# Padding the SBUF pools of a retention + maxout + bilinear kernel, so that stationary and moving operands of its matmuls start at other addresses

## The chip, the cores and the metric

The kernel runs on one core of one Trainium2 chip. The metric is the device time of one execution in microseconds. Three runs of the kernel before are given: 1272.45, 1270.91 and 1267.66 us, median 1270.91.

## What is computed

Three layers stand one behind the other, on 4608 tokens (8 batches of 576), model width 512:

```python
ret = (q @ k.T / sqrt(64)) * Dmat          # 8 heads; Dmat[i, j] = gamma_h ** (i - j) for i >= j, else 0
x = ret @ v                                 # retention; heads side by side: x is 4608 x 512
h = maximum(maximum(x @ w1, x @ w2), x @ w3)    # 512 -> 768
z = h @ w_out                               # 768 -> 512
g = (z @ u1) * (z @ u2)                     # 512 -> 1024, the second layer's w1 and w2
out = (g @ u3) @ u_out                      # 1024 -> 1024 -> 512
```

All is float32 (the weights come as float64 bits and are converted on the chip).

## The kernel before

TensorE takes the operands as float32r. For float32 accuracy each number is split into a high part (`copy_r`, L92, on ScalarE) and a low part (`low`, L95, a subtraction on VectorE or GpSimd), and each product becomes three matmuls, high x high, low x high and high x low, added up in PSUM. A matmul has a **stationary** operand of 128 x 128 (loaded into the array ahead of it by a LDWEIGHTS) and a **moving** one of 128 x 512 or 128 x 256 that is streamed through. In the profile a matmul row is named output<-moving,stationary, and the weight load has a row of its own on the queue PEld.

The program runs in five stages. Their matmuls are nearly all the work of TensorE:

1. **First products** (`products`, L478, matmul at L486), with the attention worked in between. Stationary: the tiles `w1h`/`w1l` (L197). Moving: `xh`/`xl` (L298), a block of 512 tokens; a few early ones are halved to 256 columns. 1896 matmuls of 512 columns and 96 of 256. An order written out by hand (`ORDER`) and a list of due times set the order.
2. **z** (`product`, matmul at L715, called in the loop over `z_groups`). Seven Strassen-Winograd products per group of two token blocks. Stationary: `zp["w"]` (`za11h` and so on, L545). Moving: `hh`/`hl`, split by `split_h` (L605). 504 matmuls of 512 columns; the last, half-sized group has 126 of 256.
3. **Fold** of u3 and u_out into one weight (output `ps_w`). Stationary `th`/`tl` (`get_w3t`, L720), moving `oh`/`ol` (`get_wo2`, L725), all in the pool `t34`. 192 matmuls of 512 columns.
4. **g** (outputs `ps_x`, `ps_v`, `ps_y`). Stationary: `piece` tiles of the pool `ws` (L658). Moving: two operand sets (`operand_set`, L797), set 0 in the pool `op0` on the right side of SBUF and set 1 in `op1` on the left side (L905); the token groups take them in turn. 1344 matmuls of 512 columns, half with each set, and 336 of 256 columns (the half-sized group, set 0).
5. **Out** (`add_o`, L1200). Stationary: `a11h` and so on (L1035). Moving: the folded weight's pieces. 1512 matmuls of 256 columns.

Where a tile lies in SBUF follows from the order in which pools and tiles are opened: on the left side each tile starts where the one before it ends, counted up from byte 640 of the partition; on the right side counted down from byte 229344. So an unused tile ahead of others moves them all. The kernel before has such paddings already: `skew` (L113) makes one, behind operand set 0 (L801, 352 bytes) and ahead of the stationary tiles of the stage out (L1034, 64 or 32 bytes). A half-sized group starts 48 columns into its tile (`columns`, L116), which are 192 bytes.

```python
def skew(pool, size):
    pool.tile([P, size // 4], F32, name="skew")

def columns(size):
    at = 0 if size == N1 else 48
    return slice(at, at + size)
```

Of the kernel before, what the change touches and what calls it, by code (L numbers as in the profile page):

```python
# [9 lines left out]
F32 = mybir.dt.float32  # L10
# [12 lines left out]
P = 128  # L23
# [64 lines left out]
def tile_retention_maxout_bilinear(ctx: ExitStack, tc, a, out):  # L88
# [3 lines left out]
    def copy_r(dst, src):  # L92
        nc.scalar.activation(dst, src, AF.Copy)  # L93

    def low(eng, dst, full, hi):  # L95
        eng.tensor_tensor(dst, full, hi.bitcast(F32), ALU.subtract)  # L96
# [13 lines left out]
    g_d = [dram.tile([P, KF2, N1], F32, name=f"g_d{t}") for t in range(NT // N1)]  # L110
    w4_d = dram.tile([P, KF2, DM], F32, name="w4_d")

    def skew(pool, size):  # L113
        pool.tile([P, size // 4], F32, name="skew")

    def columns(size):  # L116
        at = 0 if size == N1 else 48
        return slice(at, at + size)
# [2 lines left out]
        return ps_mm.tile([P, 512], F32, tag="mm", name=name)  # L121

    left = ctx.enter_context(ExitStack())
    hb_p = left.enter_context(tc.tile_pool(name="hb", bufs=4, side="left"))
    w1_p = left.enter_context(tc.tile_pool(name="w1", bufs=1, side="left"))
    x_p = {2: left.enter_context(tc.tile_pool(name="x2", bufs=1, side="left"))}
    cv_x = ctx.enter_context(ExitStack())
    x_p.update({t: cv_x.enter_context(tc.tile_pool(name=f"x{t}", bufs=1, side="left")) for t in range(2)})
    cv = cv_x.enter_context(tc.tile_pool(name="cv", bufs=2, side="left"))
# [372 lines left out]
    for t in range(n_blk):  # L502
        for f in range(KF1):
            for i in range(3):
                k = T_BLK * t + 3 * f + i
                if t < EARLY:
                    split = t == 0 and 3 * f + i < HALVED
                    for e, cols in enumerate(halves if split else (whole,)):
                        name = f"{t}.{3 * f + i}" + "ab"[e] * split
# [12 lines left out]
    zp = {}  # L522
# [7 lines left out]
    def splitter(pool, src, hi, lo, eng, tag, bufs):  # L530
        raw = pool.tile([P, hi.shape[-1]], F32, tag=tag, name=tag, bufs=bufs)
        load(raw, src)

        def split():
            copy_r(hi, raw)
            low(eng, lo, raw, hi)

        return split

    def open_z():  # L540
        right.close()
        cv_x.close()
        zp["ps"] = ctx.enter_context(tc.tile_pool(name="ps_2", bufs=2, space=PSUM, side="right"))
        p = zp["p"] = bx.enter_context(tc.tile_pool(name="zp", bufs=1, side="right"))
        zp["w"] = {x: [p.tile([P, KH, half], F32R, name=f"z{x}{v}") for v in "hl"] for x in AN}  # L545

    def raw_h(tag, bufs=1):
        return zp["p"].tile([P, KH, N1], F32, tag=tag, name=tag, bufs=bufs)
# [56 lines left out]
    def split_h(n):  # L605
        j, n = divmod(n, len(Z_ORDER))
        if j < len(z_groups):
            x = Z_ORDER[n][1]
            raw, size = hr[j, x], z_groups[j][3]
            hh, hl = hq[j, n] = [zp["p"].tile([P, KH, N1], F32R, tag=f"h{v}", name=f"h{v}", bufs=Z_RING)[:, :, columns(size)] for v in "hl"]  # L610
            copy_r(hh, raw)
            low(nc.vector, hl, raw, hh)

    t_last = T_BLK * (n_blk - 1)
    when(t_last, open_z)
    for c, tag in enumerate(("T3", "T2", "b21")):
        for n, step in enumerate(z_weights(c, tag)):
# [7 lines left out]
    for n in range(Z_RING):  # L625
        when(t_last + 13.6 + n, split_h, n)
    when(t_last + 15.2, load_h, 1, "b11")

    with tc.manual_schedule():
# [88 lines left out]
        t34, w3t, wo2 = {}, {}, {}  # L718
# [4 lines left out]
            return splitter(t34["p"], flat(w3t_d[:, k, 4 * e:4 * e + 4]), *map(flat, w3t[n]), nc.vector, "raw34", 3)  # L723

        def get_wo2(k):  # L725
            wo2[k] = [t34["p"].tile([P, DM], F32R, tag=x, name=x) for x in ("oh", "ol")]
            return splitter(t34["p"], wo2_d[:, k], *wo2[k], nc.gpsimd if k % 2 else nc.vector, "raw34", 3)

# [2 lines left out]
        def prepare_34(*gets):  # L731
            for split in pending:
                split()
            pending[:] = [get(n) for get, n in gets]

        first_34 = [((get_w3t, 0), (get_wo2, 0)), ((get_w3t, 1),), ((get_w3t, 2), (get_wo2, 1)), ()]

        def open_34():
            t34["p"] = t34x.enter_context(tc.tile_pool(name="t34", bufs=2, side="left"))

        zo_p = bx.enter_context(tc.tile_pool(name="zo", bufs=1, side="right"))

# [16 lines left out]
        for j, (_, _, _, size) in enumerate(z_groups):  # L759
            Z = {}  # L760
            saved = {}
            for n, (x, y) in enumerate(Z_ORDER):
                bank_of = "XVXYXYX"[n]
                fresh = bank_of not in Z
                if fresh:
                    Z[bank_of] = [bank8(f"ps_{bank_of}{i}") for i in range(2)]
                ps = Z[bank_of]
                ah, al = zp["w"][x]
                bh, bl = hq.pop((j, n))
                for i in range(2):  # L770
                    ms = slice(i * P, i * P + P)
                    product(ps[i][:, :size], [(ah[:, c, ms], al[:, c, ms], bh[:, c], bl[:, c]) for c in range(KH)], fresh, True, not fresh)
                for i in range(2):
                    if n in (0, 2, 3):
                        saved[n, i] = snap_z(ps[i], size)
                    elif n == 6:
                        keep_z(j, 2 + i, 0, ps[i])
                    else:
                        keep_z(j, *{1: (i, 0), 4: (2 + i, 1), 5: (i, 1)}[n], ps[i], saved.pop(({1: 0, 4: 3, 5: 2}[n], i)))
                split_h(j * len(Z_ORDER) + n + Z_RING)  # L780
                for fn, dj, *args in behind_z[n]:
                    fn(j + dj, *args)
                if steps and n in (2, 3, 5, 6):
                    steps.pop(0)()
            if j == 3:
                for step in steps:
                    step()
                sx.close()
                open_34()
                steps = [lambda gets=gets: prepare_34(*gets) for gets in first_34]  # L790
# [4 lines left out]
        BN = ("b11", "b21", "b22", "t1", "t2", "t3", "t4")  # L795

        def operand_set(pool, tag):  # L797
            return {x: [pool.tile([P, 2, N1], F32R, name=f"{x}{v}{tag}") for v in "hl"] for x in BN}

        ops = [operand_set(o_p, 0)]  # L800
        skew(o_p, 352)  # L801
        behind = []

# [79 lines left out]
        for n in range(2 * KF2):  # L883
            k, e = divmod(n, 2)
            th, tl = w3t.pop(n)
            for m in range(4 * e, 4 * e + 4):
                if k == 0:
                    ps_w.append(bank8(f"ps_w{m}"))
                product(ps_w[m], [(th[:, m % 4], tl[:, m % 4], *wo2[k])], k == 0, k == KF2 - 1)
                if k == KF2 - 1:  # L890
                    t = w4_p.tile([P, DM], F32, tag="w4", name="w4")
                    copy_r(t, ps_w[m])
                    load(w4_d[:, m], t)
            prepare_34(*[(get_w3t, n + 3)] * (n + 3 < 2 * KF2), *[(get_wo2, k + 2)] * (e == 1 and k + 2 < KF2))
            lows()
            if steps:
                steps.pop(0)()
# [5 lines left out]
        wk = ctx.enter_context(tc.tile_pool(name="wk", bufs=1, side="left"))  # L903
        cx = ctx.enter_context(ExitStack())
        ops.append(operand_set(cx.enter_context(tc.tile_pool(name="op1", bufs=1, side="left")), 1))  # L905

        def work(tag, bufs):
# [110 lines left out]
        def g_steps(s):  # L1018
# [13 lines left out]
            def split(x, eng):  # L1032
                if s in (0, 3) and not ops:
                    skew(gpool[s % 2], 32 if s else 64)  # L1034
                h, l = ops[x] = [gpool[s % 2].tile([P, 4, P], F32R, tag=f"{x}{v}", name=f"{x}{v}") for v in "hl"]  # L1035
                src = w[x]
                copy_r(h, src)
                if s:
                    low(eng, l, src, h)
                else:  # L1040
                    behind.append(lambda: low(eng, l, src, h))
# [58 lines left out]
        for n, (k, q) in enumerate(visits):  # L1100
            B, size = ops[k % 2], z_groups[k][3]
# [190 lines left out]
```

## Time and profile before

| what | value |
|---|---|
| runs | 1267.66, 1270.91, 1272.45 us |
| the profiled execution's own time | 1266.24 us |
| its span, first to last instruction | 1264.5 us |
| TensorE (PE) busy | 1256.5 us, 99% |
| VectorE (DVE) / ScalarE (ACT) / GpSimd (POOL) busy | 882.8 / 487.2 / 314.5 us |
| granted TensorE clock | 1.00 over the whole span |
| from where to where the stages run | first products 26 to 569 us, z to 699, fold to 744, g to 1089, out to 1264 |

A row of the chain reads: start, length, engine, output, line, number of merged instructions. Where the chain runs through matmuls alone, the length divided by the number is the time from the start of one matmul to the start of the next. A row of the timeline has a matmul's start and its own length; the lengths overlap, since the next matmul starts while the one before drains, so the difference of two starts is what a matmul costs.

### The profile page before, as it was taken

Reading aid. Unit: us, or ns where it says so; the run is one execution under the profiler, and the core shown is the slowest. Engines: PE = TensorE matmul, PEld = TensorE weight load, DVE = VectorE, ACT = ScalarE, POOL = GpSimd, SP = SyncE. Lnnn points to the kernel's source line nnn. Section 1 sums busy time; section 2 is a strip of 40 time slices with the busy share of each in tenths; the row PEclk is TensorE's granted clock in tenths of the full one; section 3 lists DMA queues with packets and bytes.
Section 4 is the critical chain, followed back from the end, with each engine's and each line's share of the span. In section 5 each row is a group of like instructions: output and inputs, shape, how many; then the busy total and the mean of one; then the engine's idle time right before and its main releaser. Section 6 shows DMA issues by size and latency. Waiting matters only on the chain.

```text
span 1264.5 us, 22993 instructions
## 1 busy us (share of the span) xinstructions
PE 1256.5 (99%) x8900; PEld 1078.9 (85%) x8900; DVE 882.8 (70%) x1256; ACT 487.2 (39%) x873; POOL 314.5 (25%) x262
## 2 busy tenths in 40 slices
PE   9999999999999999999999999999999999999999
PEld 6888888888888888888888788888998888999998
DVE  5985666666666766366898446776666766899896
ACT  4541122222222222234565354443344343455554
POOL 2201211211111110000000314544243542344443
PEclk9999999999999999999999999999999999999999
DMA  9945787787878895434743643333333315355553
GB/s 219 239 115 118 151 221 195 184 213 177 239 183 177 179 197 148 159 108 166 226 158 125 219 128 121 122 119 108 106 113 133 117 51 162 131 175 159 168 174 101
DMA packets 323793, 199.34 MB, mean 158 GB/s; under 512 B 241634, under 2 KB 279266, under 8 KB 323684
## 3 DMA queue, kind: packets, MB, share of 16 engines
q1 hardware_dynamic: 323684, 197.87, 56.7%
q8 instruction: 70, 1.15, 0.4%
q14 instruction: 39, 0.32, 0.1%
HBM read 131.76 MB, written 66.06 MB: 156 GB/s over the span
## 4 chain that ended last, share of the span: by engine, by line
PE 94%; DVE 3%; DMA 2%; ACT 1%; issue 1%; SPq 0%; POOL 0%; DVEq 0%; ACTq 0%; POOLq 0%
PE ps_h L486 35%; PE ps_x L715 23%; PE ps_y L715 11%; PE ps_v L715 6%; PE ps_X L715 5%; PE sc L369 3%; PE o L384 3%; PE ps_w L715 2%; PE ps_Y L715 2%; PE st L404 1%; PE ps_V L715 1%; PE o L391 1%; DMA raw<-w3t_d 1%; DMA a<-wp_d 1%; PE kp L345 0%
## 5 line engine op out<-in xcount | busy, mean ns | idle before, releaser
L486 PE MATMUL ps_h<-xh,w1h 128*128 128x512 f32 (+1 forms) x664 | 257.5, 389 | 0.0
L486 PE MATMUL ps_h<-xh,w1l 128*128 128x512 f32 (+1 forms) x664 | 254.4, 385 | 0.4 <-DVE w1l L96 0.4
L486 PE MATMUL ps_h<-xl,w1h 128*128 128x512 f32 (+1 forms) x664 | 174.2, 384 | 0.0
L486 PEld LDWEIGHTS ps_h<-xh,w1h 128*128 128x128 f32 x664 | 124.6, 188 | 27.6 <-issue 2.1
L486 PEld LDWEIGHTS ps_h<-xh,w1l 128*128 128x128 f32 x664 | 124.8, 188 | 24.7 <-DVE w1l L96 0.6
L486 PEld LDWEIGHTS ps_h<-xl,w1h 128*128 128x128 f32 x664 | 123.0, 188 | 24.8
L496 DVE TENSOR_TENSOR hb<-ps_h,hb 128x512 f32<-128x512 f32 (+1 forms) x110 | 74.4, 676 | 97.5 <-PE ps_h L486 92.6
L1146 POOL TENSOR_TENSOR c<-c 128x512 f32<-128x512 f32 (+1 forms) x60 | 83.4, 1391 | 176.7 <-DVE c L1138 123.3
L1133 ACT ACTIVATE snap<-ps_x 128x512 f32<-128x512 f32 (+1 forms) x100 | 55.5, 555 | 176.5 <-PE ps_x L715 175.7
L355 POOL TENSOR_TENSOR q<-q,tables 128x512 f32<-128x512 f32 (+1 forms) x31 | 31.4, 1012 | 276.4 <-DMA q<-in_q_dram 209.1
L93 ACT ACTIVATE hb<-ps_h 128x512 f32<-128x512 f32 (+1 forms) x56 | 32.5, 580 | 148.9 <-PE ps_h L486 139.1
L166 ACT ACTIVATE e<-raw 128x512 f32<-128x512 f32 x64 | 42.8, 669 | 105.8 <-DMA raw<-in_moe_w_dram 67.3
L93 ACT ACTIVATE xh<-o 128x512 fp32r<-128x512 f32 (+1 forms) x40 | 22.2, 554 | 118.8 <-PE o L391 76.9
L96 POOL TENSOR_TENSOR ol<-raw,oh 128x512 fp32r<-128x512 f32 x4 | 6.5, 1636 | 239.5 <-DVE tl L96 219.0
L358 POOL TENSOR_TENSOR v<-v,tables 128x512 f32<-128x512 f32 x40 | 44.6, 1117 | 59.9 <-DMA v<-in_v_dram 55.3
L376 DVE TENSOR_TENSOR p<-sc,mask 128x512 f32<-128x512 f32 (+1 forms) x80 | 48.0, 627 | 11.8 <-PE sc L369 11.7
L1138 DVE TENSOR_TENSOR c<-ps_x,snap 128x512 f32<-128x512 f32 (+1 forms) x40 | 25.2, 637 | 38.8 <-PE ps_x L715 15.9
L172 DVE CUSTOM_DVE_ANT_0 m<-m,r 128x1024 uint16<-128x1024 uint16 x64 | 47.0, 735 | 6.9
L1138 DVE TENSOR_TENSOR c<-ps_v,snap 128x512 f32<-128x512 f32 (+1 forms) x40 | 25.0, 635 | 35.2 <-PE ps_v L715 19.7
L715 PE MATMUL ps_x<-t4h,a 128*128 128x512 f32 (+1 forms) x160 | 45.5, 368 | 0.3 <-DVE a L96 0.3
L715 PE MATMUL ps_x<-b11h,a 128*128 128x512 f32 (+1 forms) x160 | 45.2, 367 | 0.0
L715 PE MATMUL ps_y<-b22h,s 128*128 128x512 f32 (+1 forms) x160 | 45.2, 367 | 0.0
(299 smaller groups left out, 3262.5 us busy)
## 6 DMA issues: line engine op xcount, KB each, us to landing
zr<-g_d SPq DMA_DIRECT2D x18, 1024.0 KB, 6.1
raw<-in_moe_w_dram SPq DMA_DIRECT2D x34, 512.0 KB, 5.7
g_d<-c SPq DMA_DIRECT2D x64, 256.0 KB, 2.1
zr<-z_d SPq DMA_DIRECT2D x28, 512.0 KB, 6.2
h_d<-hb SPq DMA_DIRECT2D x54, 256.0 KB, 3.4
b<-h_d SPq DMA_DIRECT2D x16, 768.0 KB, 6.6
out_dram<-ob SPq DMA_DIRECT2D x35, 256.0 KB, 2.0
v<-in_v_dram SPq DMA_DIRECT2D x32, 256.0 KB, 4.2
```

The lines of the kernel that those rows point to most:

```text
L93: nc.scalar.activation(dst, src, AF.Copy)
L166: nc.scalar.activation(z["e"], raw[:, :, 1].bitcast(F32), AF.Copy, scale=2.0 ** -112)
L172: nc.vector.tensor_tensor(z["m"], z["m"], z["r"], ALU.add)
L358: nc.gpsimd.tensor_tensor(z["v"], z["v"], vd.unsqueeze(2).to_broadcast([P, H, D]), ALU.mult)
L369: nc.tensor.matmul(z["sc"][g][keys, h, :c], z["kt"][rows, h, keys], z["qt"][rows, h, :c], start=True, stop=True)
L376: nc.vector.tensor_tensor(z[g][:c, :, :c], z["sc"][g][:c, :, :c], mask[:c, :c].unsqueeze(1).to_broadcast([c, G, c]), ALU.mult)
L486: nc.tensor.matmul(ps[:, cols], l, r, start=n == 0, stop=n == len(mms) - 1)
L496: nc.vector.tensor_tensor(hb, ps[:, cols], hb, ALU.max)
L715: nc.tensor.matmul(ps, l, r, start=start and j == 0, stop=stop and j == len(mms) - 1, skip_group_check=again)
L1133: nc.scalar.activation(t, ps[:, :size], AF.Copy)
L1138: nc.vector.tensor_tensor(r, ps[:, :size], t, ALU.add)
L1146: nc.gpsimd.tensor_tensor(x, x, y, ALU.mult)
```

## The change

Paddings (`skew`) are put into more pools, and nothing else: the built program has the same 12692 instructions, in the same order on every engine and with the same waits; only addresses in SBUF differ. `skew` itself now gives each padding its own name and one buffer, so that it can stand in a pool with several buffers.

```diff
-    def skew(pool, size):
-        pool.tile([P, size // 4], F32, name="skew")
...
+    skews = []
+
+    def skew(pool, size):
+        skews.append(pool.tile([P, size // 4], F32, name=f"skew{len(skews)}", bufs=1))
+
     hb_p = left.enter_context(tc.tile_pool(name="hb", bufs=4, side="left"))
     w1_p = left.enter_context(tc.tile_pool(name="w1", bufs=1, side="left"))
+    skew(w1_p, 64)
     x_p = {2: left.enter_context(tc.tile_pool(name="x2", bufs=1, side="left"))}
+    skew(x_p[2], 192)
...
         zp["w"] = {x: [p.tile([P, KH, half], F32R, name=f"z{x}{v}") for v in "hl"] for x in AN}
+        skew(p, 64)
...
             hh, hl = hq[j, n] = [zp["p"].tile([P, KH, N1], F32R, tag=f"h{v}", name=f"h{v}", bufs=Z_RING)[:, :, columns(size)] for v in "hl"]
+            if j == 0 and n == 0:
+                skew(zp["p"], 96)
...
         def get_wo2(k):
+            if k == 0:
+                skew(t34["p"], 192)
...
             t34["p"] = t34x.enter_context(tc.tile_pool(name="t34", bufs=2, side="left"))
+            skew(t34["p"], 192)
...
         def operand_set(pool, tag):
+            if tag:
+                skew(pool, 128)
```

What this makes of the start addresses, in bytes modulo 256 (from the addresses in the two built programs; every matmul of a line has the same two remainders):

| matmuls | count | before: moving, stationary | after: moving, stationary |
|---|---|---|---|
| first products, 512 columns | 1896 | 128, 128 | 128, 192 |
| first products, 256 columns | 96 | 128, 128 | 128, 192 |
| z, 512 | 504 | 224, 224 | 128, 64 |
| z, 256 | 126 | 160, 224 | 64, 64 |
| fold, 512 | 192 | 128, 128 | 0, 64 |
| g, 512, operand set 0 | 672 | 128, 128 | 128, 128 |
| g, 512, operand set 1 | 672 | 128, 128 | 0, 128 |
| g, 256 | 336 | 64, 128 | 64, 128 |
| out, 256 | 1512 | 128, 192 | 128, 192 |

The conversion tiles (`raw`, `e`, `r`, `m`) of the first stage move by 256 bytes; the raw tiles of z go from 224 to 128, its `zs`/`zo` tiles from 224 to 64, and `raw34` of the fold from 128 to 64.

## Rows read from the trace of the kernel before

**Rows 1.** The page: busy time of TensorE, clock by slice, the chain that ended last.
```profile
PE 1256.5 (99%) x8900; PEld 1078.9 (85%) x8900; DVE 882.8 (70%) x1256; ACT 487.2 (39%) x873; POOL 314.5 (25%) x262
...
PEclk9999999999999999999999999999999999999999
...
PE 94%; DVE 3%; DMA 2%; ACT 1%; issue 1%; SPq 0%; POOL 0%; DVEq 0%; ACTq 0%; POOLq 0%
```

**Rows 2.** Windows by stage: length, then busy PE, PEld, DVE, ACT, POOL; clock, DMA, GB/s.
```profile
40.00:100.00 60.00, 60.00 (x527) 49.39 (x524) 52.79 (x91) 31.24 (x56) 6.71 (x7) 1.00 0.66 163
...
400.00:500.00 100.00, 100.00 (x899) 83.77 (x898) 69.38 (x120) 25.05 (x44) 13.42 (x16) 1.00 0.86 186
...
567.00:690.00 123.00, 122.80 (x567) 102.41 (x566) 102.26 (x98) 66.26 (x79) 0.00 (x0) 1.00 0.50 165
690.00:745.00 55.00, 54.25 (x272) 44.98 (x271) 27.39 (x39) 26.25 (x47) 13.56 (x8) 1.00 0.61 195
745.00:1090.00 345.00, 344.71 (x1689) 292.20 (x1687) 232.05 (x308) 146.47 (x279) 145.20 (x104) 1.00 0.34 115
```

**Rows 3.** Timeline of TensorE's matmuls in the first products, 512 columns.
```profile
539.75 0.39 PE L486 MATMUL ps_h<-xh,w1h 128*128 128x512 f32 x1
539.98 0.39 PE L486 MATMUL ps_h<-xh,w1l 128*128 128x512 f32 x1
540.21 0.39 PE L486 MATMUL ps_h<-xh,w1h 128*128 128x512 f32 x1
```

**Rows 4.** The chain, in order of time: 512 columns in first products, z, fold and g.
```profile
506.60 62.79 PE ps_h L486 x276
...
635.16 4.08 PE ps_X L715 x18
...
717.65 27.04 PE ps_w L715 x118
...
799.09 5.44 PE ps_x L715 x24
```

**Rows 5.** Timeline of TensorE's matmuls in the first products, 256 columns (halved ones).
```profile
31.73 0.28 PE L486 MATMUL ps_h<-xh,w1h 128*128 128x256 f32 x1
...
32.69 0.65 PE L486 MATMUL ps_h<-xl,w1h 128*128 128x256 f32 x4
```

**Rows 6.** The chain in the stage out, 256 columns.
```profile
1125.43 2.72 PE ps_x L715 x24
1128.15 1.36 PE ps_v L715 x12
```

**Rows 7.** The chain in g, the half-sized group, 256 columns.
```profile
898.42 1.41 PE ps_v L715 x12
...
905.49 2.83 PE ps_x L715 x24
```

**Rows 8.** Timeline of TensorE's matmuls in z, the half-sized group, 256 columns.
```profile
689.73 0.28 PE L715 MATMUL ps_X<-hh,zs2l 128*128 128x256 f32 x1
...
691.97 0.28 PE L715 MATMUL ps_Y<-hl,zs1h 128*128 128x256 f32 x1
```

**Rows 9.** Timeline of the weight loads (PEld) in the first products, same place as rows 3.
```profile
539.98 0.19 PEld L486 LDWEIGHTS ps_h<-xh,w1h 128*128 128x128 f32 x1
540.21 0.19 PEld L486 LDWEIGHTS ps_h<-xh,w1l 128*128 128x128 f32 x1
```

**Rows 10.** Waits of TensorE, longest first in total: us, times, longest us.
```profile
PE warm L266 <- POOL zero L263: 1.2, 1, 1.2
PE sc L369 <- DVE qt L352: 1.0, 1, 1.0
PE o L384 <- DVE p L376: 0.5, 2, 0.4
PE ps_h L486 <- DVE w1l L96: 0.4, 1, 0.4
```

## The prediction
> **What bounds the kernel now.** I read the page first. TensorE is busy for 1256.5 of the 1264.5 us, the chain that ended last is 94% TensorE, and its clock is granted in full in every slice [rows 1], which is the 2.4 GHz level. The waits of TensorE come to some 3 us at the head of the list, most of them single waits near the start [rows 10]. So nothing but the matmuls' own pace decides, and a nanosecond on each of several thousand matmuls goes straight into the time. The question is what a matmul costs from start to start, and whether it depends on the addresses of its operands.
>
> **What a matmul costs.** The chain, where it runs through matmuls alone, gives this by division [rows 4]: first products 62.79 / 276 = 227.5 ns, z 4.08 / 18 = 226.7, g 5.44 / 24 = 226.7, fold 27.04 / 118 = 229.2 (with a few waits inside). I take 226.7 for 512 columns; the timeline says the same, 230 ns by rounded starts [rows 3]. In all these the moving and the stationary operand start at the same byte modulo 256 (the table of the change).
>
> For 256 columns four kinds of pairs are there. Moving 128 and stationary 128: eight matmuls from 31.73 to 32.69, 120.0 ns [rows 5]. Moving 64, stationary 128: 1.41 / 12 = 117.5 and 2.83 / 24 = 117.9 [rows 7]. Moving 160, stationary 224: nineteen matmuls from 689.73 to 691.97, 117.9 [rows 8]. Moving 128, stationary 192: 2.72 / 24 = 113.3 [rows 6]. So the same shape with the same number of columns goes at 113.3 to 120.0 ns, and the address pair is what I can find to tell them apart.
>
> Is the difference there at 512 columns too? With equal remainders 512 columns cost 226.7 and 256 cost 120.0: the 256 columns between them take 106.7 ns, which is one column per tick of 2.4 GHz. What is left, 226.7 - 213.3 = 13.4 ns at 512 and 120.0 - 106.7 = 13.3 at 256, is a fixed cost per matmul at equal remainders. With the pair 128, 192 it is 113.3 - 106.7 = 6.6. The weight load of a matmul starts with the stream of the matmul before it: the load at 539.98 and the matmul at 539.98 start together [rows 3, 9]. A load is as long for 512 columns as for 256, so a collision of its reads with the stream's would cost the same in both. This is why I carry 120.0 - 113.3 = **6.7 ns per matmul** over from 256 to 512 columns. No row shows a 512-column matmul with unequal remainders, so this step is an inference; its bounds are 0 (the fixed cost is something else) and 13.4 (all of it goes).
>
> **The change, part by part.** No instruction is added, removed or moved, no wait and no transfer; the sum has only matmuls, count times price.
>
> - First products: 1896 x 6.7 = 12.7 us, and the 96 halved ones 0.6 us. Their new pair, 128 and 192, is the very pair of the stage out.
> - z, 512 columns: 504 x 6.7 = 3.4 us. The new pair, moving 128 and stationary 64, is not in the trace. It lies 64 bytes below where the pair of the stage out lies 64 above. Bounds 0 and 3.4 from the rows; I take the full price because modulo 128 it is the same pair as in the stage out.
> - Fold: 192 x 6.7 = 1.3 us, pair 0 and 64, as above. Some of this can be lost: TensorE already idles 0.75 of 55 us there [rows 2].
> - g, operand set 1: 672 matmuls go from 128, 128 to 0, 128. A distance of 128 is in no row. Nothing (the remainders modulo 128 are equal) and 672 x 6.7 = 4.5 us are the ends. The rows at part of the price (117.5 to 117.9, some 2 ns better than equal remainders) are nearest to the middle, and I take half, 2.3 us.
> - z, half-sized group: 126 matmuls of 256 columns go from the pair 160, 224 to 64, 64, equal remainders. They lose up to 120.0 - 117.9 = 2.1 ns each, 0.3 us; I take 0.2 as loss.
> - g set 0, the half-sized group of g and the stage out keep their pairs: nothing.
> - Other engines and transfers: the moved tiles are also read and written by VectorE, ScalarE and the DMA queues. I cost this at nothing, because TensorE covers it: VectorE's highest shares are 52.79 of 60 us early on and 102.26 of 123 us in z, the DMA engines' 0.86 [rows 2]. With TensorE some 3% faster VectorE's shares become about 0.91 and 0.86, below one; if single waits appear early, the 215 first products that stand between 40 and 100 us have no more than 215 x 6.7 = 1.4 us to lose. In g VectorE has 232 of 345 us and is not near.
>
> Sum: 12.7 + 0.6 + 3.4 + 1.3 + 2.3 - 0.2 = 20.1 us. Against the profiled execution's own time this is 1266.2 - 20.1 = 1246.1 us. That execution lies 4.7 us below the median of the three runs, so for a median I count from there: 1270.9 - 20.1 = **1250.8**, 1.6% faster. (About 0.5%, some 6.4 us, is what a measurement of this kernel can tell from no change.)
>
> A rule of the Trainium skill speaks against all of this. The page "TensorE: Matmul & The Clock Gate", section "Step-by-step: what each phase is for", says that TensorE reads SBUF through two independent ports, one for the moving operand and one for the weight load, so that loading the next weights takes no read bandwidth from the running matmul. By that rule addresses would not matter and the sum would be 0; the trace does not agree at 256 columns, where the pair 128, 192 has 113.3 ns and 128, 128 has 120.0 [rows 5, 6], and is silent at 512. The same section gives about 216 ns from start to start for a 512-column matmul; by that figure an estimate of the most to be won would be 226.7 - 216, near 11 ns per matmul, where I take 6.7.
>
> **The rivals.**
>
> 1. *Only the pair that the trace shows helps.* First products gain 12.7 + 0.6 us; z, the fold and set 1 stay at 226.7. For it: the rows 117.5 and 117.9 also have 64 bytes between their operands and yet win only 2 of the 6.7 ns [rows 7, 8], so the distance alone does not decide. Against it: those rows have moving operands that start off a multiple of 128, and all the new pairs do not. 1270.9 - 13.3 = 1257.6 us.
> 2. *It does nothing measurable.* The fixed 13.4 ns at 512 columns is a start-up cost that no address touches; the difference among the 256-column matmuls would then come from the load, which there fills nearly the whole stream (a load is 0.19 us long, a matmul starts every 0.113 to 0.120) and at 512 has time to spare. Weight loads are busy 102.41 of 123 us in z [rows 2], so they have gaps at 512 columns. Against it: the cost is the same 13.3 and 13.4 at both widths, which would be chance. The two-port rule of the Trainium skill (page and section above) would end here too. 1271 us; with a remainder of 2.1 ns on the 2592 matmuls of 512 columns, as rows 7 and 8 have, 1265.
> 3. *Slower: at 512 columns unequal remainders collide more.* With equal remainders load and stream start in step; set apart, they could meet again in the second half of a long stream, which no 256-column row can show. The price would be the same 6.7 ns with the other sign on the 1896 + 504 + 192 = 2592 matmuls, 17.4 us: 1288 us. It decides from 2.5 ns per matmul on (6.4 us / 2592). Against it: a load is 0.19 us long and starts with the stream [rows 9], which at 512 columns leaves little of it to the second half, and no 256-column pair is dearer than the equal one.
>
> **How the numbers follow.** Forecast 0.64, rival 1 0.14, rival 2 0.16, rival 3 0.06. Faster by over 0.5%: forecast and rival 1, 0.78. Within 0.5%: rival 2, 0.16. Slower: rival 3, 0.06. The range begins at 1243: the forecast counted from the profiled execution, 1246.1, with the full price for set 1, 2.2 less, and 1 us towards a price above 6.7. It ends at 1267: past rival 1 (1257.6) and the partial gain of 1265 that rival 2 holds, with 1.5 us for the spread above the median (1272.45 - 1270.91). Left out are the rest of rival 2 and rival 3.
>
> **What would show it.** In the changed kernel's chain, first products at about 220 ns from start to start (the row of some 276 matmuls before z at near 60.7 us in place of 62.79), z and fold near 220, g in two kinds of stretches, 226.7 with set 0 and something between 220 and 226.7 with set 1, and out unchanged at 113.3; the span of the stage up to z shorter by some 13 us, and the 256-column tail of z at 118 to 120. Wrong would be: first products still at 226.7 (rival 2) or above 229 (rival 3), z and fold at 226.7 while first products are faster (rival 1), or TensorE waiting for VectorE in z where it does not now.

## The result and the profile after

The changed kernel takes 1281.44 us (median of four runs, 1281.29 to 1287.4), the kernel before, run beside it, 1269.29: ratio 1.0114, 95% interval 1.0087 to 1.0141. It is **slower by 1.1%**; forecast was 1.6% faster. The profiled execution has 1281.33 us and a span of 1279.6, 15.1 more than before.

The page of the changed kernel answers to [rows 1]: TensorE alone has grown, by 16.2 us; the other engines are within 1.4 us of what they were, and the clock is granted in full in both.

```profile
PE 1272.7 (99%) x8900; PEld 1078.3 (84%) x8900; DVE 882.7 (69%) x1256; ACT 487.6 (38%) x873; POOL 313.1 (24%) x262
...
PEclk9999999999999999999999999999999999999999
...
PE 98%; DVE 0%; DMA 0%; ACT 0%; issue 0%; POOL 0%; POOLq 0%; ACTq 0%; DVEq 0%
```

Where it went is read in the chain, in order of time (start, length, what, number of matmuls), to be set against [rows 4]:

```profile
514.78 64.59 PE ps_h L491 x276
...
616.47 4.12 PE ps_X L723 x18
...
728.46 27.80 PE ps_w L723 x118
...
772.60 5.44 PE ps_x L723 x24
...
811.15 5.60 PE ps_x L723 x24
```

Per matmul: first products 64.59 / 276 = 234.0 ns (before 227.5), z 228.9 (226.7), fold 235.6 (229.2), g with operand set 0 226.7 as before, g with set 1 5.60 / 24 = 233.3 (226.7). Wherever the operands of 512-column matmuls were set apart these got slower; set 0, left alone, did not. In the first products two costs take turns, 231 and 236 ns by the unrounded starts, 233.3 in the mean without the waits; the timeline, which rounds, has 230 and 240:

```profile
548.65 0.39 PE L491 MATMUL ps_h<-xh,w1l 128*128 128x512 f32 x1
548.88 0.40 PE L491 MATMUL ps_h<-xh,w1h 128*128 128x512 f32 x1
549.12 0.39 PE L491 MATMUL ps_h<-xh,w1l 128*128 128x512 f32 x1
549.35 0.40 PE L491 MATMUL ps_h<-xh,w1h 128*128 128x512 f32 x1
```

By the first matmul of each stage in the two traces the stages grew by 10.0 us up to z, 0.9 in z, 0.7 in the fold, 3.5 in g and 0.0 in out, together the 15.1 us of the span. VectorE is not part of it: in z it has 101.63 of 123 us where it had 102.26 [rows 2].

### The profile page after: what moved, and what is told of

Read it like the earlier page. It is cut to its first block, busy times and chain, and to the rows that moved or that the text cites. A ratio compares the mean times of both kernels' runs of the same rounds, so it can differ in the third digit from the quotient of the medians.

```text
span 1279.6 us, 22993 instructions
## 1 busy us (share of the span) xinstructions
PE 1272.7 (99%) x8900; PEld 1078.3 (84%) x8900; DVE 882.7 (69%) x1256; ACT 487.6 (38%) x873; POOL 313.1 (24%) x262
## 4 chain that ended last, share of the span: by engine, by line
PE 98%; DVE 0%; DMA 0%; ACT 0%; issue 0%; POOL 0%; POOLq 0%; ACTq 0%; DVEq 0%
PE ps_h L491 36%; PE ps_x L723 23%; PE ps_y L723 11%; PE ps_X L723 6%; PE ps_v L723 6%; PE ps_w L723 3%; PE ps_Y L723 3%; PE sc L374 3%; PE o L389 3%; PE ps_V L723 1%; PE st L409 1%; PE o L396 1%; PE kp L350 0%; DMA raw<-wo_d 0%; PE qp L350 0%
## 5 line engine op out<-in xcount | busy, mean ns | idle before, releaser
L491 PE MATMUL ps_h<-xh,w1h 128*128 128x512 f32 (+1 forms) x664 | 260.8, 394 | 0.0
L491 PE MATMUL ps_h<-xh,w1l 128*128 128x512 f32 (+1 forms) x664 | 257.8, 390 | 0.0
L491 PE MATMUL ps_h<-xl,w1h 128*128 128x512 f32 (+1 forms) x664 | 178.1, 390 | 0.0
L381 DVE TENSOR_TENSOR p<-sc,mask 128x512 f32<-128x512 f32 (+1 forms) x80 | 48.0, 626 | 12.1 <-PE sc L374 12.0
L723 PE MATMUL ps_v<-b21h,a 128*128 128x512 f32 (+1 forms) x160 | 45.5, 369 | 0.0
```

Source lines behind the costliest of these rows:

```text
L381: nc.vector.tensor_tensor(z[g][:c, :, :c], z["sc"][g][:c, :, :c], mask[:c, :c].unsqueeze(1).to_broadcast([c, G, c]), ALU.mult)
L491: nc.tensor.matmul(ps[:, cols], l, r, start=n == 0, stop=n == len(mms) - 1)
L723: nc.tensor.matmul(ps, l, r, start=start and j == 0, stop=stop and j == len(mms) - 1, skip_group_check=again)
```

## The experiments

I call **distance** the stationary operand's start minus the moving one's, modulo 256 bytes. The changed pairs have distance 64 (first products, fold), 192 (z) and 128 (set 1). In the code of the sweeps, as it is shown here, the expressions that make the blocks' names are shortened to `name`.

### TensorE alone, all distances

```diff
+    for width, dm, ds in PAIRS:              # start bytes modulo 256: moving, stationary
+        ps = block(name, width, dm, ds, 24)
...
+        for j in range(count):
+            m = j // 2 % 4 * 512 + dm // 4
+            s = j * 3 % 16 * 128 + ds // 4
+            nc.tensor.matmul(ps[:, :width], st[:, s:s + P], mv[:, m:m + width], start=j == 0, stop=j == count - 1)
```

> This kernel computes nothing of the reference: it loads part of q, runs blocks of 24 matmuls on it with TensorE alone, and stores one result many times. The blocks differ in the width (512, 384, 320 or 256 columns) and in the start bytes modulo 256 of the moving and the stationary operand. Theory A (the collision of the weight load with the stream depends on the distance of the two start addresses and on the width): at 512 columns and moving 128, stationary 128 about 227 ns from start to start, stationary 192 about 233.5, stationary 64 about 229, stationary 0 (distance 128) about 233; at 256 columns 120 with equal remainders and 113 with stationary 192; equal remainders at 0, 64 and 224 all about 227. Theory B (the loss at 512 columns comes from other engines or transfers that meet the moved tiles): with TensorE alone all blocks of 512 columns have about 227 ns, or all about 220. Theory C (a stationary operand off a multiple of 128 is dear at 512 columns, whatever the moving one): the blocks with stationary 64 and 192 are dear at every moving remainder, those with moving 64 and stationary 64 too.

The chain has one row per block of 24. The first letter of a name is the width (w 512, n 256), the second the start of the moving operand and the third that of the stationary one (a is 0, one letter is 16 bytes: e is 64, i 128, m 192, o 224). In the blocks of 320 columns (l) the letters are the same.

```profile
70.70 3.52 PE lii L39 x24
...
77.73 3.52 PE lim L39 x24
...
107.52 2.87 PE nii L39 x24
...
118.90 2.72 PE nim L39 x24
...
130.18 5.58 PE wia L39 x24
...
152.47 5.51 PE wie L39 x24
...
169.18 5.46 PE wih L39 x24
174.64 5.44 PE wii L39 x24
180.08 5.45 PE wij L39 x24
...
196.71 5.59 PE wim L39 x24
...
219.08 5.46 PE waa L39 x24
...
230.13 5.60 PE wae L39 x24
...
274.76 5.45 PE wee L39 x24
...
347.32 5.45 PE woo L39 x24
```

At 512 columns equal remainders give 5.44 to 5.46 / 24, near 227 ns, at every place (wii, waa, wee, woo), and so do distances 16 and 240 (wij, wih). Distance 64 gives 5.59 / 24 = 233 (wim, and wae from another place), 128 gives 232.5 (wia), 192 gives 229.6 (wie). At 256 columns it is the other way round: distance 0 has 119.6 (nii) and distance 64 has 113.3 (nim), the cheapest there. At 320 columns all eight distances of the sweep cost the same 3.52 / 24 = 146.7 (lii and lim are two of them), and at 384 they lie between 173.3 and 176.7. Theory A holds in every number. B falls, since no other engine works here and the rows differ as in the kernel; C falls by wee, whose stationary operand starts at 64 and which costs 227.

### The change without the paddings of the first products

```diff
     w1_p = left.enter_context(tc.tile_pool(name="w1", bufs=1, side="left"))
-    skew(w1_p, 64)
     x_p = {2: left.enter_context(tc.tile_pool(name="x2", bufs=1, side="left"))}
-    skew(x_p[2], 192)
```

> The change without its two paddings of the first products (their pair goes back to 128, 128), all else as changed. By the sums of the steps in the two traces the first products lose 11.5 us at 512 columns and win 1.1 at 256 by the change. Theory A: they go back to 227 ns, the time falls by about 10.4 us from 1281.4 to about 1271. Theory B (something else moved along, and the first products are slow for another reason): less than half of it, above 1276.

1276.17 us, ratio 1.0065 to before (1.0048 to 1.0083). By the sum alone this is where theory B put it, and my number for A was missed; the chain tells why. The first products are back at 62.78 / 276 = 227.5 ns, and z starts 10.2 us earlier than in the changed kernel (569.0 against 579.2). But the stage out, whose instructions and addresses nobody touched, goes at another pace:

```profile
506.40 62.78 PE ps_h L489 x276
...
1180.09 2.83 PE ps_x L721 x24
1182.91 1.41 PE ps_v L721 x12
```

It has 2.83 / 24 = 117.9 ns where [rows 6] had 113.3, and over 1512 matmuls this is near 6 us. So 10 us were won and 6 lost by something new. One of the four runs took 1272.69 us, near theory A's 1271; which pace its stage out had is not known, since there is a trace of the first run alone (1276.75).

### The same tiles moved, the operands together

```diff
     skew(w1_p, 64)
...
-    skew(x_p[2], 192)
...
-        skew(p, 64)
...
-            if k == 0:
-                skew(t34["p"], 192)
...
             if tag:
-                skew(pool, 128)
+                skew(pool, 256)
```

> The change with other sizes: nearly all the tiles that the change moves are moved again, but both operands together, so that every pair of 512 columns has equal remainders (first products 192 and 192, z 128 and 128, fold 64 and 64, set 1 at 128 and 128). Theory A (only the distance of the two start addresses counts): all matmuls of 512 columns at about 227 ns, the time as before, 1266 to 1272 us, with some 5 us open for the 256-column stretches that were seen at 113 or 118 ns at one and the same distance. Rival (the new places themselves, or what else is read and written there, cost the time): above 1276 us, with first products above 230 ns.

1266.22 us against 1266.46 of the kernel before, ratio 1.0004 (0.9984 to 1.0023). The chain has first products at 62.78 / 276 again, at 192 and 192, and z at 226.7, at 128 and 128:

```profile
507.07 62.78 PE ps_h L490 x276
...
607.31 4.08 PE ps_X L721 x18
```

So neither the moving of tiles nor what else reads and writes at the new places costs the time by itself. With the sweep, where TensorE works alone and four places give the same costs at the same distance, that leaves the distance.

### TensorE alone, with a stop ahead of each block

```diff
-    ps_p = ctx.enter_context(tc.tile_pool(name="ps", bufs=8, space=PSUM))
+    ps_p = ctx.enter_context(tc.tile_pool(name="ps", bufs=1, space=PSUM))
...
+        if rep:
+            nc.tensor.matmul(ps[:, :256 + 20 * rep], st[:, :P], mv[:, :256 + 20 * rep], start=True, stop=True)
         for j in range(count):
...
+        nc.scalar.activation(o[:cols, :64], ps[:cols, :64], AF.Copy)    # the next block's bank waits for this
```

> Computes nothing of the reference: blocks of 16 matmuls with TensorE alone at the 16 distances in steps of 16 bytes, at 256 and at 512 columns, eight blocks of each; TensorE stands still ahead of each block, and one matmul of 256 to 396 columns goes ahead of seven of the eight, so that each block begins at another moment. Theory A1 (at 256 columns and distance 64 the pace can lock in one of two ways, and a stop of TensorE decides which): some of the eight blocks at 113 ns and some at 118; at 512 columns and distances 0 and 16 all at 227. Rival (the two paces at 256 columns come from other engines): all eight at 113. If a 512-column block anywhere has about 220, there is a pair better than equal remainders.

The moving operand starts at 128 here; the second letter of a name is the start of the stationary one (m is 192) and the last letter one of the eight starts (a to h). Timeline at 256 columns and distance 64 (nm), four of the eight blocks; in front of the 16 stands the one matmul that shifts the start, behind an idle time of 0.37 us (one is shown).

```profile
284.67 1.99 PE L42 MATMUL nmrc<-mv,st 128*128 128x256 f32 x16
287.03 0.41 PE L38 MATMUL nmrd<-mv,st 128*128 128x316 f32 x1 [0.37 <-ACT o L43]
287.29 1.98 PE L42 MATMUL nmrd<-mv,st 128*128 128x256 f32 x16
289.90 2.05 PE L42 MATMUL nmre<-mv,st 128*128 128x256 f32 x16
...
297.89 2.05 PE L42 MATMUL nmrh<-mv,st 128*128 128x256 f32 x16
```

Same addresses, same matmuls: 1.98 to 1.99 us in two, 2.05 in the two others; by the last ten steps from start to start of each, 113.3 to 113.4 ns in six of the eight blocks and 117.7 to 117.8 in two. A1 holds for 256 columns: at distance 64 a stream falls into one of two paces (I say it locks), with no other engine at work. The start seems to decide which: the run over other widths below has the first four starts again and gives 113.3 to 113.4 in all four, as here. Distance 192 reached 113.3 as well, in one of its eight blocks; the seven others had 117.7 to 117.9. At 512 columns distance 64 had 233.3 to 233.4 in all eight blocks; distance 0 had 226.6 to 229.2, a little more than expected, distance 240 much the same, 226.6 to 228.5, and distance 16 233 in seven of eight, so the good spell at 16 in the first sweep was one lock of two. No block of 512 columns came below 226.6: none of the 16 distances, with eight starts each, is better than equal remainders.

### Shorter weight loads

```diff
-            nc.tensor.matmul(ps[:, :width], st[:, s:s + P], ...
+            nc.tensor.matmul(ps[:cols, :width], st[:, s:s + cols], ...    # cols 128, 64, 32
```

> Computes nothing of the reference: blocks of 16 matmuls with TensorE alone, with stationary operands of 128, 64 and 32 columns, at eight distances in steps of 32 bytes and at 256 and 512 columns. Theory A (the weight load's reads of SBUF meet the stream's): a shorter load meets it less, so the spread over the distances at 512 columns (227 to 234 with 128 stationary columns, some 7 ns) and the 13 ns above 213 shrink with 64 and 32 columns. Rival (a cost of starting a stream, which has nothing to do with the load's reads): the spread and the 13 ns stay the same with 64 and 32 columns.

Timeline, blocks of 16 matmuls of 512 columns, second of two: with 128 stationary columns at distance 0 and 64, with 64 columns at 0 and 64, with 32 columns at 0 and 32. The loads were 188, 134 and 108 ns long with 128, 64 and 32 columns.

```profile
184.88 3.81 PE L42 MATMUL wferb<-mv,st 128*128 128x512 f32 x16
...
202.55 3.88 PE L42 MATMUL wfgrb<-mv,st 128*128 128x512 f32 x16
...
255.07 3.84 PE L42 MATMUL wherb<-mv,st 128*64 128x512 f32 x16
...
272.57 3.86 PE L42 MATMUL whgrb<-mv,st 128*64 128x512 f32 x16
...
324.86 3.87 PE L42 MATMUL wqerb<-mv,st 128*32 128x512 f32 x16
333.61 3.97 PE L42 MATMUL wqfrb<-mv,st 128*32 128x512 f32 x16
```

Neither theory came out whole. The cost above 213 does not shrink with the load, as A had it; the least over the distances is 226.7 with each of the three lengths, as the rival had it, and with 32 columns one block is the dearest of all, (3.97 - 0.40) / 15 = 238 ns. But which distance is cheap did not stay, against the rival. Distance 0, best at 128 columns (227), loses that at 64 (230) and 32 (232). At 256 columns of stream and a load of 64, distance 0 has 113.3 to 113.4 ns in both blocks, where with 128 it had 119.3 to 119.5; distance 64 reaches 113.3 in one of two. There are only two starts per block, and with fewer stationary columns the matmul also writes fewer rows of its output, so it is not shown that the load's length alone does this. What inside TensorE or SBUF makes the cost stays open.

### One part alone

```diff
+    skew(w1_p, 64)
...
+    skew(x_p[2], 192)
```

> The kernel before with the two paddings of the first products alone (moving 128, stationary 192), z, the fold and set 1 as before. Theory A (the price hangs on the distance and is paid in each stage by itself): first products at 231 and 236 ns in turn, 1873 x 6.8 = 12 us dearer, some 1 us back at 256 columns; 1277 to 1278 us, with 5 us more where the stage out locks at 118 ns. Rival (the loss arises where stages with different distances stand together): less than half of it, below 1273 us.

1277.36 us against 1269.39, ratio 1.0072 (1.0044 to 1.0099). The chain shows the first products dear as in the changed kernel and z behind them at 226.7 as before:

```profile
514.83 64.59 PE ps_h L491 x276
...
583.53 4.08 PE ps_V L720 x18
```

64.59 / 276 = 234.0 ns, as in the changed kernel. z starts at 579.3 us, 10.0 later than before. Theory A holds: each stage pays for its own distance.

### Other widths

```diff
-CASES = [(name, w, 128, 16 * e, P, r) for w in (256, 512) for e in range(16) for r in range(8)]
+CASES = [(name, w, 128, 16 * e, P, r) for w in (192, 240, 256, 272, 288, 320, 352, 384, 416, 448, 480, 496, 512)
+         for e in (8, 12, 4, 0) for r in range(4)]
```

> Computes nothing of the reference: blocks of 16 matmuls with TensorE alone, widths from 192 to 512 columns, at distances 0, 64, 192 and 128, four blocks of each with another start. Theory Q (the cost above one column per tick comes in steps of 6.7 ns; a stream of up to 256 columns can get by with one step, a longer one needs two at least): at distance 64 one step (7 ns above the columns' own time) up to 256 columns, and two or three from 272 on; at distance 0 two steps at all widths. Rival (my forecast's law: a fixed cost that only the addresses set): the cost above the columns' own time at distance 64 stays near 7 ns up to 496 columns. Rival (a smooth growth with the width): the cost at distance 64 grows evenly from 7 ns at 256 columns to 20 at 512.

The first letter of a name is the width (b is 240, c 256, d 272, e 288, f 320, k 480, m 512), the second the start of the stationary operand as above. Timeline, one block each: at distance 64 with 240 to 320 and with 512 columns, and at distance 0 with 480 (kirc):

```profile
77.92 1.95 PE L42 MATMUL bmrc<-mv,st 128*128 128x240 f32 x16
...
119.29 1.99 PE L42 MATMUL cmrc<-mv,st 128*128 128x256 f32 x16
...
161.95 2.16 PE L42 MATMUL dmrc<-mv,st 128*128 128x272 f32 x16
...
206.68 2.29 PE L42 MATMUL emrc<-mv,st 128*128 128x288 f32 x16
...
253.85 2.50 PE L42 MATMUL fmrc<-mv,st 128*128 128x320 f32 x16
...
527.28 3.63 PE L42 MATMUL kirc<-mv,st 128*128 128x480 f32 x16
...
681.80 3.90 PE L42 MATMUL mmrc<-mv,st 128*128 128x512 f32 x16
```

Above the columns' own time (columns / 2.4, last ten steps) distance 64 costs 12 ns at 240 columns (13.8 in one block), 6.7 at 256, 10 at 272, 13.4 at 288 and 320, 14.7 to 16.7 at 384, 13.4 again at 416, 15 at 448, 16 at 480, 13.3 at 496 (20 in one block) and 20 at 512. All three laws fall: it is no fixed cost, no rule of one step up to 256 columns, and no even growth. The cheap lock at distance 64 belongs to 256 columns, and it is gone 32 columns further on. Distance 0 is no fixed cost either: near 13 ns at 256 and from 320 to 384, but 11.4 to 12.1 at 272 and 288, 16 at 448 and 16.7 at 480. Nor is it the cheapest at every long width: at 448 distance 192 has 13.4, and at 480 distance 128 has 13.3 in three of four blocks.

## Why the prediction was wrong

1. **What bounds the kernel** was right. TensorE's own pace decides: it grew by 16.2 us and the span by 15.1.
2. **That a matmul's cost depends on the operands' addresses** was right: with TensorE alone wii has 5.44 us per block and wim 5.59. The rule of two independent ports in the Trainium skill ("TensorE: Matmul & The Clock Gate", section "Step-by-step: what each phase is for"), taken as the prediction took it, would have given no difference; the two blocks do not agree with that.
3. **The step that failed is the price**: 6.7 ns per matmul, carried from 256 to 512 columns. The argument was that 13.4 ns at 512 and 13.3 ns at 256, both at equal remainders, are one fixed cost, of which the pair 128, 192 takes off half. But what a pair takes off at one width says nothing about another: at distance 64 the cost is 6.7 at 256 columns, 10 at 272, 13.4 at 288 and 20 at 512. Rival 2 had called the equality chance; in part it was, since distance 0 itself goes from 11.4 to 17 ns at widths between. At 512 columns 226.7 is the least that any distance gave; the pair 128, 192 costs 233.3 there, 6.6 more instead of 6.7 less.
4. **The reading of [rows 6 to 8]** was wrong as well. I took 113.3, 117.5 and 117.9 ns for three address pairs and, against rival 1, made "moving at a multiple of 128" the difference. All three have distance 64; they are the two locks of one distance. The trace of before held the proof: the half-sized group of g runs at 117.8 in [rows 7], up to a stop at 926 us, and at 1.36 / 12 = 113.3 behind it. The stage out does the same at one address pair: it begins at 117.8 (1090.52, 12 matmuls in 1.41 us) and goes at 113.3 in [rows 6]. The chain of before, just after the stop at 926 us and at the beginning of out:

```profile
926.39 2.21 PE ps_x L715 x17
928.61 1.36 PE ps_v L715 x12
...
1090.52 1.41 PE ps_v L715 x12
```

5. Term by term, forecast gain against measured loss: first products 13.3 against a loss of 10.0 (11.6 at 512 columns; 1.1 won back at 256, fewer waits included; the first of them started 0.5 us earlier); z 3.4 against 0.9, tail included (its pair, distance 192, is not that of the stage out, as I took it modulo 128); fold 1.3 against 0.7; set 1 2.3 against 672 x 6.6 = 4.4 lost, of which 1.0 came back in the half-sized group, which happened to take the cheap lock. The z tail, at equal remainders, went from 117.9 to 120.0 as forecast, though that it stood on the dearer of the two paces before was luck. Out kept its length. The losses of the stages come to 15.1 us, where a gain of 20.1 was forecast.
6. **The rivals.** Rival 3 came true, with the sign, place and price it was given (6.7 ns) on first products and fold; in z, at distance 192, it is 2.2, and set 1, which it left out, pays 6.6 as well. Its reason, that load and stream meet again in the second half of a long stream, is not shown. It gave 1288 where 1281.4 was measured, and had a chance of 0.06. I had set it low because no 256-column pair was dearer than the equal one, which is the same false step: the order of the pairs at one width says nothing about another.

## What to carry to other kernels

Where TensorE is bound by its stream of weight loads and matmuls, the start of the stationary operand relative to the moving one, modulo 256 bytes, can be worth some 3% of each float32r matmul of 512 columns (226.7 against 233.3 ns) and 6% at 256 (113.3 against 120.0), and nothing at 320 (146.7 at every distance tried). A sweep with TensorE alone measures it for one's own width in one run, if each block is started in several ways. A price found at one width is not to be used at another: 64 bytes apart is the best distance here at 256 columns and one of the worst at 512, where no distance is better than equal remainders. When rows of one shape differ, look first whether they differ within one stage, around a stop, before putting it down to addresses.

## What the runs showed of the hardware that I had not expected

- At 256 columns and distance 64 the stream has two paces, 113.3 and 117.8 ns, each held over hundreds of matmuls. A break in the stream could change the pace: the stage out of the changed kernel goes at 117.8 up to two steps of 161 and 222 ns at 1125 us, then at 113.3, and that of the kernel before changed at 1100 us behind one step of 125 ns. Or it did not: in the run without the paddings of the first products the same place has steps of 154 and 222 ns, and all 1512 matmuls go at 117.8, which costs about 6 us. The chain around that place in the changed kernel, then in the run without the paddings of the first products:

```profile
1123.96 1.41 PE ps_v L723 x12
1125.37 1.52 PE ps_x L723 x12
1126.90 1.36 PE ps_y L723 x12
```

```profile
1113.52 1.41 PE ps_v L721 x12
1114.93 1.55 PE ps_x L721 x12
1116.49 1.41 PE ps_y L721 x12
```

- At 512 columns the cost takes turns within one stream, 231 and 236 ns at distance 64, and 226, 229 and 232 at distance 192, with nothing else at work.
- No experiment gave a version faster than the kernel before: it already has equal remainders at 512 columns and distance 64 in the long 256-column stage.
